# Last 64 queries of two attention heads in one block of 128 rows

## The chip, the cores and the metric

The kernel runs on one core of one Trainium2 chip. The metric is the time of one execution in microseconds (us). The kernel before takes 1045.41 us, the median of three runs (1045.2 to 1045.7).

## The reference

Attention with a decay bias feeds two MLPs. There are 4 batches, 8 heads, 576 positions and 64 channels per head.

```python
cum = np.cumsum(np.maximum(s, 0.0), axis=-1)
bias = -(cum[:, :, :, None] - cum[:, :, None, :])
scores = np.where(causal, -1e9, scale * q @ k.T + np.minimum(bias, 0.0))
attn = np.exp(scores - max); attn = attn / (attn.sum(-1) + 1e-9)
x = (attn @ v) as 2304 tokens of 512
h = x @ w_in;  g = maximum(h, 0) + log1p(exp(-abs(h)));  x = g @ w_out
h = x @ w_in2; g = P(h) / (Q(h) + 1e-6);                 out = g @ w_out2
```

P is a cubic and Q a quadratic in h and |h|; each MLP is 512 to 2048 to 512.

## The kernel before

**Order of the work.** The two MLPs are cut into units of one token tile and 128 of the 2048 inner columns. The first MLP has six token tiles T=0 to 5 (`T1`: 256, 256 and four of 448 tokens), the second six of 384. A loop over the units (L1269) issues for each unit the first product (`stage_a`, L1006 to L1008: three matmuls per 128 rows, since every operand is split into a high and a low part), the nonlinearity (`stage1` to `stage3`), and three units later the second product (`stage_b`, L1042 to L1044 in the first MLP, L1049 to L1051 in the second). Attention runs between the units: `gap` spreads a list of attention steps (`stream`) over the units, in four groups (`GROUPS`), so that each token tile of the first MLP has its attention rows before it starts. Attention ends just before T=4.

**Who sets the order.** All instructions of the first 600 us are put in order, engine by engine, by a planner (`Planner`, `plan`, L1335): a list scheduler over modelled durations that takes the time by which an operation must be done as its rank. What is issued later keeps the order of the tile framework.

**Attention of one head.** A part of kind H (there are 32, one per head and batch) covers queries 384 to 575 of a head, in two blocks of softmax rows. The first (`s1`) is queries 384 to 511, 128 rows against 512 keys. The second (`s2`) is queries 448 to 575, 128 rows against 576 keys, of which only the last 64 rows are used. The parts of kinds L, M and B cover earlier queries. For the second block of one head:

- `scores` (L609, L610) makes two blocks of 288 keys in two PSUM banks, two matmuls each;
- `softmax_rows` adds the mask and takes the row minimum of the negated scores in two DVE operations (L593, L596), the exponent with its row sum on ACT (L600, 128x576), the reciprocal in two small DVE operations (L601, L602) and the scaling on POOL (L603, 128x576), all in the tile `P4`, of which there is one buffer;
- `t2` turns rows 64 to 127 by five transposes of 64 rows (L694), and `evac_pt` takes them from PSUM to SBUF: for batch 0 by one DVE copy (L657), for the others as a high part on ACT (L660) and a low part on DVE (L661);
- `pv` (L732) multiplies by the values and adds the result to the tile of tokens (L743, or L746 and L747).

The turned rows lie in two pairs of tiles `pth`, `ptl` (or `pt` for batch 0), taken in turn by the number of the part (`p.idx % 2`).

```python
for i, k0 in enumerate((448, 0, 128, 256, 384)):
    nc.tensor.transpose(bk[:, (i + 1) * 64:(i + 2) * 64], p.p2[64:128, k0:k0 + 128], ident[64:128, 64:128])
```

**PSUM.** There are eight banks: four for the sums (`acc`), two for `stage_a` (`h`) and two for attention (`at`). `hsel` (L1013) gives the units of T=4 and of most of the second MLP the `h` and `at` banks in turn.

The order of the steps in `stream`, for part number i: load of part i+2, `s1` of i, `pv` of i-2, preparation of the next part, `t1` and `t2` of i-1, `s2` of i.

Of the kernel before, what the change touches and what calls it, by code (L numbers as in the profile page):

```python
# [23 lines left out]
NF = DFF // 128  # L24
# [7 lines left out]
H_ONLY = 5  # L32
# [299 lines left out]
def moe_chain_kernel(ctx, tc, qk0, v0, qk, vv, s0, s, w1, w2, ab, out):  # L332
    nc = tc.nc
# [11 lines left out]
        return sb.tile(shape, dt, tag="W", bufs=NF, name=name)  # L345

    def t_j(name, shape, dt):
        return sb.tile(shape, dt, tag="J", bufs=4, name=name)

    def t_r(name, shape, dt):  # L350
        return sb.tile(shape, dt, tag="R", bufs=2, name=name)
# [1 line left out]
    def t_l(name, shape, dt):  # L353
        return sb.tile(shape, dt, tag="Lw", bufs=8, name=name)
# [10 lines left out]
    def tmp_tile(tag, bufs, shape=(128, TMAX), dt=F32):  # L365
        return sb.tile(list(shape), dt, tag=tag, bufs=bufs, name=tag)
# [13 lines left out]
    def f(ap):  # L380
        return ap.bitcast(F32)
# [4 lines left out]
    abt, nega, babs, qc = prm[:, 0:6], prm[:, 6:10], prm[:, 10:12], prm[:, 12:13]  # L386


    pt_h, pt_l = [], []
    x_t = {}  # L390
    v_t = {}
    raw_t = {}
# [2 lines left out]
    class Part:  # L395
        def __init__(self, b, h, kind, rng, first, plain, pv_plain):
            self.b, self.h, self.kind, self.rng = b, h, kind, rng
            self.fresh, self.first, self.plain, self.pv_plain = rng is not None, first, plain, pv_plain

    def cols(t, rng):  # L400
        if rng[0] == "pre":
# [182 lines left out]
    def softmax_rows(pt, bk, q0, n, stat, i, second=None):  # L584
        mo = 512 - n
        if second is None:
            nc.vector.tensor_tensor_reduce(  # L587
                out=pt[:, 0:n], in0=bk[:, 0:n], in1=mask[:, mo:mo + n], scale=-0.125,
                scalar=3.0e38, op0=ALU.add, op1=ALU.min, accum_out=stat[:, i, 0:1])
            mn = stat[:, i, 0:1]  # L590
        else:
            hn = n // 2
            nc.vector.tensor_tensor_reduce(  # L593
                out=pt[:, 0:hn], in0=bk[:, 0:hn], in1=mask[:, 0:hn], scale=-0.125,
                scalar=3.0e38, op0=ALU.add, op1=ALU.min, accum_out=stat[:, i, 3:4])
            nc.vector.tensor_tensor_reduce(  # L596
                out=pt[:, hn:n], in0=second[:, 0:hn], in1=mask[:, 512 - hn:512], scale=-0.125,
                scalar=stat[:, i, 3:4], op0=ALU.add, op1=ALU.min, accum_out=stat[:, i, 0:1])
# [12 lines left out]

    at_bank = [lambda: bank("at")]

    def abank():
        return at_bank[0]()
# [22 lines left out]
    def s2(p):  # L638
        if p.kind in "LB":
            p.p2 = p_tile(p, "gl")  # L640
            bk = abank()
            scores(bk[:, 0:384], p, 256, 0, 384)
            softmax_rows(p.p2, bk, 256, 384, p.stat, 2)
        elif p.kind == "H":
            p.p2 = tmp_tile("P4", 1, (128, S))
            bk = abank()
            scores(bk[:, 0:288], p, 448, 0, 288)
            bk2 = abank()
            scores(bk2[:, 0:288], p, 448, 288, 288)
            softmax_rows(p.p2, bk, 448, 576, p.stat, 1, second=bk2)  # L650
# [12 lines left out]
    def t1(p):  # L663
        if p.pv_plain:
            p.pt = (sb.tile([128, 960], F32, tag="pt", bufs=2, name="pt"),)
        else:
            p.pt = (pt_h[p.idx % 2], pt_l[p.idx % 2])
        if p.kind == "B":
            return
        bk = abank()  # L670
        if p.kind in "LM":
            for i, c0 in enumerate((256, 0, 128)):
                nc.tensor.transpose(bk[:, i * 128:(i + 1) * 128], p.p1[:, c0:c0 + 128], ident)
            evac_pt([t[:, 0:384] if p.first else t[:, 192:576] for t in p.pt], bk[:, 0:384], nc.scalar)
        else:
            for c in range(4):
                nc.tensor.transpose(bk[:, c * 128:(c + 1) * 128], p.p1[:, c * 128:(c + 1) * 128], ident)
            o = 64 if p.pv_plain else 256
            evac_pt(
                [t[:, o:o + 768].rearrange("p (c q) -> p c q", c=4)[:, :, 0:128] for t in p.pt],  # L680
                bk.rearrange("p (c q) -> p c q", c=4), nc.scalar)

    def t2(p):
        if p.kind == "M":
            return
        bk = abank()
        if p.kind in "LB":
            for i in range(3):
                nc.tensor.transpose(bk[:, i * 128:(i + 1) * 128], p.p2[:, i * 128:(i + 1) * 128], ident)
            evac_pt([t[:, 0:384] if p.pv_plain else t[:, 576:960] for t in p.pt], bk[:, 0:384])  # L690
        else:
# [3 lines left out]
            evac_pt(  # L695
                [t.rearrange("p (c q) -> p c q", c=5)[:, :, 0:64] if p.pv_plain else
                 t[:, 64:1024].rearrange("p (c q) -> p c q", c=5)[:, :, 128:192] for t in p.pt],
                bk[:, 64:384].rearrange("p (c q) -> p c q", c=5))

    def pv(p):  # L700
        if p.first:
            pv_first(p)
            return
        bk = abank()
        hd = p.h % 2
        ops = []
# [66 lines left out]
    }  # L773

    def parts_of(lst, first=False, plain=False, pv_plain=False):
        return [Part(b, h, k, r, first, plain, pv_plain) for b, heads, kind in lst for h in heads for k, r in SPLIT[kind]]

    R8 = range(8)
    segs = [
# [15 lines left out]
    n = 0  # L795
# [131 lines left out]
    def home2(ff, half):  # L927
        if ff >= 14:
            return t_l("w2h", [128, 512], F32R), t_l("w2l", [128, 512], F32R)
        if ff not in w2_t:  # L930
            al = t_j if ff < 2 else t_q if ff < 5 else t_v if ff < 6 else t_w
# [79 lines left out]
    hcnt = [0]  # L1011

    def hsel(ph, T, ff):  # L1013
        if (ph == 0 and T != 4) or (ph == 1 and T == 0 and ff < H_ONLY):
            return "h"
        hcnt[0] += 1
        return ("h", "at")[hcnt[0] % 2]

    def open_acc(ph, T):
        both = ph == 0 and T < 2  # L1020
        n = 2 if both else KD if ph == 0 else TILES[ph][T][1] // 128
        tags = ("at", "at", "acc", "acc") if (ph, T) == (0, 5) else ("acc",) * n
        acc_t[ph, T] = [bank(t) for t in tags]
        if both:
            for a in acc_t[ph, T]:
                nc.tensor.matmul(a, pt_h[0][:, 0:128], w1_t[0][:, 0:512], start=True, stop=False)

    def stage_b(u):
        ph, T, ff = u
# [68 lines left out]
    def stage1_(u):  # L1098
# [11 lines left out]
        else:  # L1110
            a = tmp_tile("e", 2)[:, 0:n]
            t = tmp_tile("PA", 3, (128, n))
            w = tmp_tile(*(("P4", 1), ("tc", 3), ("tmp", 1), ("tc", 3))[(T * NF + ff) % 4], (128, n))
# [36 lines left out]
    if True:  # L1150
# [118 lines left out]
        for i in range(NU + LAGS[1]):  # L1269
# [42 lines left out]
            if u is not None:  # L1312
                gap(i, 1)
                t4 = i - 4 * NF
                if t4 == 0:
                    for lst in (pt_h, pt_l, v_t, op_t, allp, stream):
                        lst.clear()
                if 0 < t4 <= 20:
                    conv2_to(t4)
# [76 lines left out]
```

## Time and profile before

| what | value |
|---|---|
| median of three runs | 1045.41 us |
| the profiled execution | 1044.85 us |
| its span in the profile | 1043.1 us |
| PE busy | 98% of the span |
| ACT, DVE, POOL busy | 77%, 75%, 44% of the span |
| granted TensorE clock | full speed (2.4 GHz) in all 40 slices |

PE is TensorE's matmuls, PEld its weight loads, DVE VectorE, ACT ScalarE, POOL GpSimd. The span is from the first to the last instruction of the profile; 1.75 us of the profiled execution lie outside it. Matmuls are pipelined, and their ends in the profile are modelled: the time that one takes from its engine is read from start to start.

### The profile page before, as it was taken

The numbers are of one execution on the slowest core, as the hardware profiler recorded it, in microseconds if no ns is written. First come the engines' busy times: TensorE is split into PE (matmuls) and PEld (weight loads), VectorE is DVE, ScalarE is ACT, GpSimd is POOL, SyncE is SP. The second block draws the span as 40 slices with busy tenths as digits, with TensorE's granted clock in tenths as the row PEclk, the third lists the DMA queues.
The fourth block names the chain that finished last, engine by engine and source line by source line (L and its number), as shares of the span: only waits on it lengthen the run. The fifth ranks groups of instructions, "written<-read, shape, count | busy, mean of one in ns | idle before, by whom it ended". The sixth has DMA issues, their size and how long they took to land.

```text
span 1043.1 us, 17736 instructions
## 1 busy us (share of the span) xinstructions
PE 1018.0 (98%) x5764; PEld 923.3 (89%) x5764; DVE 784.5 (75%) x1858; ACT 803.5 (77%) x1693; POOL 459.4 (44%) x509
## 2 busy tenths in 40 slices
PE   6999999999999999999999999999999999999998
PEld 5889989988998888999999999989999999999996
DVE  5888877788887888885776787687676776767765
ACT  5898878887887778786566567778787887887875
POOL 2756765421221122222435775445454454444542
PEclk9999999999999999999999999999999999999999
DMA  8877566565564644435779865010010110100100
GB/s 237 298 244 240 171 211 209 176 202 155 167 180 129 207 151 139 129 107 175 246 231 324 301 181 194 1 31 31 1 62 1 31 31 1 44 18 1 31 1 31
DMA packets 67950, 138.70 MB, mean 133 GB/s; under 512 B 8336, under 2 KB 21456, under 8 KB 67856
## 3 DMA queue, kind: packets, MB, share of 16 engines
q1 hardware_dynamic: 65312, 133.39, 40.6%
q10 hardware_dynamic: 2544, 4.16, 1.5%
q8 instruction: 46, 0.75, 0.3%
q14 instruction: 48, 0.39, 0.1%
HBM read 110.82 MB, written 22.61 MB: 128 GB/s over the span
## 4 chain that ended last, share of the span: by engine, by line
PE 71%; DVE 12%; ACT 6%; DMA 4%; POOL 3%; issue 3%; SPq 0%; POOLq 0%; DVEq 0%; ACTq 0%
PE h L1007 6%; PE h L1006 6%; PE h L1008 6%; PE at L732 5%; PE acc L1049 5%; PE acc L1051 5%; PE acc L1050 5%; PE acc L1043 4%; PE acc L1042 4%; PE acc L1044 4%; PE at L1006 3%; PE at L1007 3%; PE at L1008 3%; PE at L609 3%; PE at L610 2%
## 5 line engine op out<-in xcount | busy, mean ns | idle before, releaser
L1006 PE MATMUL h<-xs,w1h 128*128 128x448 f32 (+1 forms) x352 | 120.1, 342 | 1.3 <-DVE e L1108 1.3
L1043 PE MATMUL acc<-gl,w1h 128*128 128x448 f32 (+1 forms) x352 | 119.4, 341 | 1.2 <-POOL gl L1146 1.2
L1007 PE MATMUL h<-xs,w1h 128*128 128x448 f32 (+1 forms) x352 | 119.5, 340 | 0.0
L1008 PE MATMUL h<-xs,w1l 128*128 128x448 f32 (+1 forms) x352 | 119.4, 340 | 0.0
L1042 PE MATMUL acc<-gh,w1h 128*128 128x448 f32 (+1 forms) x352 | 119.3, 341 | 0.0
L1044 PE MATMUL acc<-gh,w1l 128*128 128x448 f32 (+1 forms) x352 | 118.2, 338 | 0.1
L603 POOL TENSOR_SCALAR PA<-PA,stat 128x384 f32<-128x384 f32 (+3 forms) x112 | 71.9, 648 | 101.5 <-DVE stat L602 33.6
L1049 PE MATMUL acc<-w2h,gh 128*128 128x512 f32 x288 | 113.9, 395 | 0.1
L1051 PE MATMUL acc<-w2h,gl 128*128 128x512 f32 x288 | 113.5, 394 | 0.0
L1050 PE MATMUL acc<-w2l,gh 128*128 128x512 f32 x288 | 113.5, 394 | 0.0
L1146 POOL TENSOR_TENSOR gl<-PA,gh 128x384 fp32r<-128x384 f32 x95 | 96.7, 1018 | 6.2 <-ACT gh L1144 5.0
L1117 POOL TENSOR_TENSOR tc<-tc,e 128x384 f32<-128x384 f32 x47 | 50.8, 1082 | 98.5 <-ACT tc L1115 98.5
L603 POOL TENSOR_SCALAR P<-P,stat 128x576 f32<-128x576 f32 x32 | 26.4, 824 | 136.2 <-DVE stat L602 36.0
L600 ACT ACTIVATE PA<-PA,stat 128x384 f32<-128x384 f32 (+3 forms) x112 | 64.0, 572 | 11.5 <-DVE stat L587 9.3
L1006 PEld LDWEIGHTS h<-xs,w1h 128*128 128x128 f32 x352 | 66.3, 189 | 5.4 <-DVE e L1108 1.7
L1043 PEld LDWEIGHTS acc<-gl,w1h 128*128 128x128 f32 x352 | 66.1, 188 | 4.7 <-POOL gl L1146 1.4
L1007 PEld LDWEIGHTS h<-xs,w1h 128*128 128x128 f32 x352 | 66.2, 188 | 3.3
L1008 PEld LDWEIGHTS h<-xs,w1l 128*128 128x128 f32 x352 | 66.2, 188 | 3.3
L1044 PEld LDWEIGHTS acc<-gh,w1l 128*128 128x128 f32 x352 | 66.1, 189 | 3.4 <-POOL w1l L882 0.3
L1042 PEld LDWEIGHTS acc<-gh,w1h 128*128 128x128 f32 x352 | 66.1, 189 | 3.2
L1051 PEld LDWEIGHTS acc<-w2h,gl 128*128 128x128 f32 x288 | 54.1, 188 | 13.1 <-DVE gl L1146 0.3
L1130 DVE SCALAR_TENSOR_TENSOR tc<-tc,e 128x384 f32<-128x384 f32 x48 | 27.5, 574 | 50.4 <-ACT e L1129 48.6
(235 smaller groups left out, 3209.0 us busy)
## 6 DMA issues: line engine op xcount, KB each, us to landing
w1l<-l_d SPq DMA_DIRECT2D x138, 256.0 KB
raw<-in_w_dram SPq DMA_DIRECT2D x48, 512.0 KB
raw<-in_qk_dram SPq DMA_DIRECT2D x24, 384.0 KB
l_d<-w1l SPq DMA_DIRECT2D x32, 256.0 KB
raw64x<-in_w_dram SPq DMA_DIRECT2D x16, 512.0 KB
raw<-in_qk_dram SPq DMA_DIRECT2D x8, 576.0 KB
w_d<-PA SPq DMA_DIRECT2D x16, 256.0 KB
R<-in_vv_dram SPq DMA_DIRECT2D x12, 320.0 KB
```

The lines of the kernel that those rows point to most:

```text
L600: nc.scalar.activation(pt[:, 0:n], pt[:, 0:n], AF.Exp, bias=mn, scale=-1.0, accum_out=stat[:, i, 1:2])
L603: nc.gpsimd.tensor_scalar(pt[:, 0:n], pt[:, 0:n], stat[:, i, 2:3], 1.0, op0=ALU.mult, op1=ALU.mult)
L1006: nc.tensor.matmul(h, wh[:, cs], xh, start=(k == 0), stop=False)
L1007: nc.tensor.matmul(h, wh[:, cs], xl, start=False, stop=False)
L1008: nc.tensor.matmul(h, wl[:, cs], xh, start=False, stop=(k == KD - 1))
L1042: nc.tensor.matmul(o, wh[:, cs], gh, start=first and not both, stop=False)
L1043: nc.tensor.matmul(o, wh[:, cs], gl, start=False, stop=False)
L1044: nc.tensor.matmul(o, wl[:, cs], gh, start=False, stop=last and (not both or m % 2 == 1))
L1049: nc.tensor.matmul(acc[m], gh[:, cs], wh, start=first, stop=False)
L1050: nc.tensor.matmul(acc[m], gh[:, cs], wl, start=False, stop=False)
L1051: nc.tensor.matmul(acc[m], gl[:, cs], wh, start=False, stop=last)
L1146: eng.tensor_tensor(gl, g, f(gh), op=ALU.subtract)
```

## The change

The even head of a pair puts its queries 512 to 575 in rows 0 to 63 of a block, and the odd head its own in rows 64 to 127 of the same block. Each head still has its own four score matmuls and two mask operations, the latter on its 64 rows alone. The exponent, the reciprocal, the scaling and the transposes are done once for both heads; the five transposes take all 128 rows, four into one bank and one into another. `pv` of the even head is done with that of the odd one. The tiles `pth`, `ptl` and `pt` hold both heads (`p.h % 2`); `P4` has two buffers instead of one. The first four units of T=4 take only `h` banks.

```diff
@@ fill
-        for i in range(2):
-            for lst, nm in ((pt_h, "pth"), (pt_l, "ptl")):
-                t = t_j(nm, [128, 1024], F32R)
-                nc.gpsimd.memset(f(t[:, 0:192]), 0.0)
-                lst.append(t)
+        for lst, nm in ((pt_h, "pth"), (pt_l, "ptl")):
+            t = t_j(nm, [128, 2, 1024], F32R)
+            nc.gpsimd.memset(f(t[:, :, 0:192]), 0.0)
+            lst.append(t)
@@ softmax_rows
             hn = n // 2
+            r = slice(0, 64) if q0 == 512 else slice(64, 128)
+            mo = q0 - hn - 64 if q0 == 512 else 512 - hn
             nc.vector.tensor_tensor_reduce(
-                out=pt[:, 0:hn], in0=bk[:, 0:hn], in1=mask[:, 0:hn], scale=-0.125,
-                scalar=3.0e38, op0=ALU.add, op1=ALU.min, accum_out=stat[:, i, 3:4])
+                out=pt[r, 0:hn], in0=bk[r, 0:hn], in1=mask[r, 0:hn], scale=-0.125,
+                scalar=3.0e38, op0=ALU.add, op1=ALU.min, accum_out=stat[r, i, 3:4])
...
             mn = stat[:, i, 0:1]
+            if q0 == 512:
+                return
@@ scores
-        nc.tensor.matmul(o, p.ht[:, 0, q0:q0 + 128], p.ht[:, 1, k0:k0 + n], start=True, stop=False)
-        nc.tensor.matmul(o, p.st[0:68, 0, q0:q0 + 128], p.st[0:68, 1, k0:k0 + n], start=False, stop=True)
+        hq, sq = (t.rearrange("p a s -> p (a s)")[:, q0:q0 + 128] for t in (p.ht, p.st))
+        nc.tensor.matmul(o, hq, p.ht[:, 1, k0:k0 + n], start=True, stop=False)
+        nc.tensor.matmul(o, sq[0:68], p.st[0:68, 1, k0:k0 + n], start=False, stop=True)
@@ s2
-            p.p2 = tmp_tile("P4", 1, (128, S))
+            if p.mate is None:
+                p.p2 = tmp_tile("P4", 2, (128, S))
+                p.stat2 = sb.tile([128, 1, 4], F32, tag="stat2", bufs=2, name="stat2")
+            else:
+                p.p2, p.stat2 = p.mate.p2, p.mate.stat2
+            q0 = 512 if p.mate is None else 448
             bk = abank()
-            scores(bk[:, 0:288], p, 448, 0, 288)
+            scores(bk[:, 0:288], p, q0, 0, 288)
...
@@ t1
-            p.pt = (pt_h[p.idx % 2], pt_l[p.idx % 2])
+            p.pt = (pt_h[0][:, p.h % 2], pt_l[0][:, p.h % 2])
@@ t2
-            for i, k0 in enumerate((448, 0, 128, 256, 384)):
-                nc.tensor.transpose(bk[:, (i + 1) * 64:(i + 2) * 64], p.p2[64:128, k0:k0 + 128], ident[64:128, 64:128])
...
+        elif p.mate is not None:
+            n, ts = (0, pt_p) if p.pv_plain else (128, (pt_h[0], pt_l[0]))
...
+            bk = abank()
+            for i in range(4):
+                nc.tensor.transpose(bk[:, i * 128:(i + 1) * 128], p.p2[:, i * 128:(i + 1) * 128], ident)
+            evac_pt([t[:, :, 1:5] for t in ts], bk.rearrange("p (c j q) -> p j c q", c=4, j=2))
+            bk = abank()
+            nc.tensor.transpose(bk[:, 0:128], p.p2[:, S - 128:S], ident)
+            evac_pt([t[:, :, 0] for t in ts], bk[:, 0:128].rearrange("p (j q) -> p j q", j=2))
@@ pv
+        if p.kind == "H":
+            if p.mate is None:
+                return
+            pv_later(p.mate)
+        pv_later(p)
@@ hsel
-        if (ph == 0 and T != 4) or (ph == 1 and T == 0 and ff < H_ONLY):
+        if (ph == 0 and (T != 4 or ff < 4)) or (ph == 1 and T == 0 and ff < H_ONLY):
             return "h"
```

The rest of the diff follows from these: `t_j` has two buffers of twice the size, the weights `w2` of the second MLP that later take their place are cut in the same way, and `parts_of` gives each odd head its mate.

## Rows read from the trace of the kernel before

**Rows 1.** Page, busy time and share of the span, instructions.

```profile
PE 1018.0 (98%) x5764; PEld 923.3 (89%) x5764; DVE 784.5 (75%) x1858; ACT 803.5 (77%) x1693; POOL 459.4 (44%) x509
```

**Rows 2.** Busy time by stretch: stretch, length, engines' busy us, clock, DMA share, GB/s.

```profile
0.00:60.00 60.00, 47.55 (x265) 40.12 (x266) 41.76 (x178) 44.18 (x129) 31.82 (x57) 1.00 0.86 266
60.00:200.00 140.00, 133.26 (x1043) 127.93 (x1042) 113.00 (x309) 117.49 (x279) 84.20 (x85) 1.00 0.63 201
200.00:476.00 276.00, 275.92 (x1665) 246.52 (x1664) 226.98 (x714) 221.71 (x505) 63.80 (x102) 1.00 0.53 158
476.00:620.00 144.00, 144.00 (x713) 133.03 (x712) 98.26 (x139) 84.94 (x158) 75.55 (x69) 1.00 0.80 258
```

**Rows 3.** Waits of PE from 60 to 200 us: total us, times, longest.

```profile
PE at L689 <- POOL PA L603: 3.0, 5, 0.8
PE at L694 <- POOL P L603: 2.5, 4, 1.1
```

**Rows 4.** Timeline of PE around one group of five transposes of 64 rows.

```profile
212.10 0.36 PE L1008 MATMUL h<-xs,w1l 128*128 128x448 f32 x1
212.30 0.36 PE L1006 MATMUL h<-xs,w1h 128*128 128x448 f32 x1
212.59 0.52 PE L694 MATMUL at<-ident,P 64*128 64x64 f32 x5
213.04 0.47 PE L1007 MATMUL h<-xs,w1h 128*128 128x448 f32 x1
213.35 0.37 PE L1008 MATMUL h<-xs,w1l 128*128 128x448 f32 x1
```

**Rows 5.** Timeline of PE around four transposes of 128 rows, and around one.

```profile
217.17 0.60 PE L677 MATMUL at<-ident,PA 128*128 128x128 f32 x4
217.52 0.45 PE L1008 MATMUL h<-xs,w1l 128*128 128x448 f32 x1
217.81 0.36 PE L1006 MATMUL h<-xs,w1h 128*128 128x448 f32 x1
...
299.21 0.36 PE L1008 MATMUL h<-xs,w1l 128*128 128x448 f32 x1
299.42 0.27 PE L689 MATMUL at<-ident,PA 128*128 128x128 f32 x1
299.44 0.42 PE L609 MATMUL at<-ht 128*128 128x384 f32 x1
299.70 0.34 PE L610 MATMUL at<-st 68*128 68x384 f32 x1
299.88 0.38 PE L689 MATMUL at<-ident,PA 128*128 128x128 f32 x2
```

**Rows 6.** Groups by line, PE: the transposes of 64 rows; count, busy us, mean ns.

```profile
L694 PE MATMUL at<-ident,P 64*128 64x64 f32 x160 | 17.6, 234 | 2.7 <-POOL P L603 2.5
```

**Rows 7.** Groups by line, 60 to 476 us: the other engines' operations around the block.

```profile
L603 POOL TENSOR_SCALAR P<-P,stat 128x576 f32<-128x576 f32 x32 | 26.4, 824 | 136.2 <-DVE stat L602 36.0 <-DVE stat L601 32.8 <-PE at L677 21.3
L600 ACT ACTIVATE P<-P,stat 128x576 f32<-128x576 f32 x32 | 24.5, 765 | 1.9 <-DVE stat L596 1.3 <-ACT ht L564 0.5
L602 DVE RECIPROCAL stat<-stat 128x1 f32<-128x1 f32 x128 | 19.2, 155 | 1.5
L601 DVE TENSOR_SCALAR stat<-stat 128x1 f32<-128x1 f32 x127 | 17.8, 145 | 5.8 <-ACT PA L600 4.3 <-ACT P L600 0.2
L661 DVE TENSOR_TENSOR ptl<-at,pth 128x512 fp32r<-128x512 f32 x24 | 16.5, 688 | 4.2 <-ACT pth L660 3.5
L660 ACT ACTIVATE pth<-at 128x512 fp32r<-128x512 f32 x24 | 14.3, 596 | 1.2 <-PE at L677 0.6
L747 DVE TENSOR_TENSOR x<-at,tmp 64x192 f32<-64x192 f32 x23 | 8.0, 349 | 0.5 <-ACT tmp L746 0.2
L746 ACT ACTIVATE tmp<-at 64x192 f32<-64x192 f32 x23 | 7.5, 326 | 2.3 <-PE at L732 1.8
```

**Rows 8.** Timeline of PE: the first matmul of T=4, next after attention's last.

```profile
476.87 0.37 PE L1006 MATMUL at<-xs,w1h 128*128 128x448 f32 x1
```

More of the change, by code (lines that the diff above doesn't have):

```diff
@@ L347, in t_j @@
     def t_j(name, shape, dt):
-        return sb.tile(shape, dt, tag="J", bufs=4, name=name)
+        return sb.tile(shape, dt, tag="J", bufs=2, name=name)
     def t_r(name, shape, dt):
@@ L592, in softmax_rows @@
             hn = n // 2
+            r = slice(0, 64) if q0 == 512 else slice(64, 128)
+            mo = q0 - hn - 64 if q0 == 512 else 512 - hn
             nc.vector.tensor_tensor_reduce(
-                out=pt[:, 0:hn], in0=bk[:, 0:hn], in1=mask[:, 0:hn], scale=-0.125,
-                scalar=3.0e38, op0=ALU.add, op1=ALU.min, accum_out=stat[:, i, 3:4])
+                out=pt[r, 0:hn], in0=bk[r, 0:hn], in1=mask[r, 0:hn], scale=-0.125,
+                scalar=3.0e38, op0=ALU.add, op1=ALU.min, accum_out=stat[r, i, 3:4])
             nc.vector.tensor_tensor_reduce(
-                out=pt[:, hn:n], in0=second[:, 0:hn], in1=mask[:, 512 - hn:512], scale=-0.125,
-                scalar=stat[:, i, 3:4], op0=ALU.add, op1=ALU.min, accum_out=stat[:, i, 0:1])
+                out=pt[r, hn:n], in0=second[r, 0:hn], in1=mask[r, mo:mo + hn], scale=-0.125,
+                scalar=stat[r, i, 3:4], op0=ALU.add, op1=ALU.min, accum_out=stat[r, i, 0:1])
             mn = stat[:, i, 0:1]
+            if q0 == 512:
+                return
         nc.scalar.activation(pt[:, 0:n], pt[:, 0:n], AF.Exp, bias=mn, scale=-1.0, accum_out=stat[:, i, 1:2])
@@ L644, in s2 @@
         elif p.kind == "H":
-            p.p2 = tmp_tile("P4", 1, (128, S))
+            if p.mate is None:
[4 more added lines that the diff above has]
+            q0 = 512 if p.mate is None else 448
             bk = abank()
-            scores(bk[:, 0:288], p, 448, 0, 288)
+            scores(bk[:, 0:288], p, q0, 0, 288)
             bk2 = abank()
-            scores(bk2[:, 0:288], p, 448, 288, 288)
-            softmax_rows(p.p2, bk, 448, 576, p.stat, 1, second=bk2)
+            scores(bk2[:, 0:288], p, q0, 288, 288)
+            softmax_rows(p.p2, bk, q0, 576, p.stat2, 0, second=bk2)
     def evac_pt(dst, src, eng=None):
@@ L664, in t1 @@
         if p.pv_plain:
-            p.pt = (sb.tile([128, 960], F32, tag="pt", bufs=2, name="pt"),)
+            if not pt_p:
+                pt_p.append(sb.tile([128, 2, 960], F32, name="pt"))
+            p.pt = (pt_p[0][:, p.h % 2],)
         else:
-            p.pt = (pt_h[p.idx % 2], pt_l[p.idx % 2])
+            p.pt = (pt_h[0][:, p.h % 2], pt_l[0][:, p.h % 2])
         if p.kind == "B":
@@ L690, in t2 @@
             evac_pt([t[:, 0:384] if p.pv_plain else t[:, 576:960] for t in p.pt], bk[:, 0:384])
-        else:
-            for i, k0 in enumerate((448, 0, 128, 256, 384)):
-                nc.tensor.transpose(bk[:, (i + 1) * 64:(i + 2) * 64], p.p2[64:128, k0:k0 + 128], ident[64:128, 64:128])
[L695 to L698, printed above, removed]
+        elif p.mate is not None:
+            n, ts = (0, pt_p) if p.pv_plain else (128, (pt_h[0], pt_l[0]))
+            ts = [t[:, :, 0:960] if p.pv_plain else t[:, :, 64:1024] for t in ts]
+            ts = [t.rearrange("p j (c q) -> p j c q", c=5)[:, :, :, n:n + D] for t in ts]
+            bk = abank()
[5 more added lines that the diff above has]
+            evac_pt([t[:, :, 0] for t in ts], bk[:, 0:128].rearrange("p (j q) -> p j q", j=2))
     def pv(p):
@@ L775, in parts_of @@
     def parts_of(lst, first=False, plain=False, pv_plain=False):
-        return [Part(b, h, k, r, first, plain, pv_plain) for b, heads, kind in lst for h in heads for k, r in SPLIT[kind]]
+        out, mates = [], {}
+        for b, heads, kind in lst:
+            for h in heads:
+                for k, r in SPLIT[kind]:
+                    p = Part(b, h, k, r, first, plain, pv_plain)
+                    p.mate = mates.get((b, h - 1, k)) if h % 2 else None
+                    mates[b, h, k] = p
+                    out.append(p)
+        return out
     R8 = range(8)
@@ L929, in home2 @@
             return t_l("w2h", [128, 512], F32R), t_l("w2l", [128, 512], F32R)
+        if ff < 2 and ff not in w2_t:
+            t = t_j("w2", [128, 2, 1024], F32R)
+            w2_t[ff] = (t[:, 0], t[:, 1])
         if ff not in w2_t:
-            al = t_j if ff < 2 else t_q if ff < 5 else t_v if ff < 6 else t_w
+            al = t_q if ff < 5 else t_v if ff < 6 else t_w
             w2_t[ff] = (al("w2h", [128, 1024], F32R), al("w2l", [128, 1024], F32R))
@@ L1025, in open_acc @@
             for a in acc_t[ph, T]:
-                nc.tensor.matmul(a, pt_h[0][:, 0:128], w1_t[0][:, 0:512], start=True, stop=False)
+                nc.tensor.matmul(a, pt_h[0][:, 0, 0:128], w1_t[0][:, 0:512], start=True, stop=False)
     def stage_b(u):
@@ L1315, in moe_chain_kernel @@
                 if t4 == 0:
-                    for lst in (pt_h, pt_l, v_t, op_t, allp, stream):
+                    for lst in (pt_h, pt_l, pt_p, v_t, op_t, allp, stream):
                         lst.clear()
```

6 lines of the change are left out of this document (4 added, 2 removed).

## The prediction

> **What bounds the kernel now.** I read the page's busy shares first, then busy time by stretch, then PE's own waits, then PE's timeline around single groups of transposes. The page shows PE busy 98% of the span, the next engine 77% [rows 1]. Such a share is an average, so the stretches decide [rows 2]. In the first 60 us PE is busy 47.55 us and the DMA engines 0.86: that is the start, and the loads bound it. From 60 to 200 us PE is busy 133.26 of 140 us while ACT (117.49) and DVE (113.00) are nearly full too: a mixed bound, in which PE waits now and then, mostly for POOL's scaled rows ahead of a transpose, 3.0 and 2.5 us in all [rows 3]. From 200 to 476 us PE is busy 275.92 of 276 us and waits for nothing, though DVE and ACT have 49 and 54 us to spare. So from 200 us on only what leaves PE's own queue shortens the kernel. The clock is full in every stretch.
>
> A busy PE says little of what one matmul costs it, since records overlap. So the price of a transpose is read from start to start, with the matmuls on both sides.
>
> **The change part by part.**
>
> *Transposes of 64 rows, removed.* The matmuls of 448 columns start 0.20 us apart (212.10, 212.30) [rows 4]. From the start of the last one before the group (212.30) to the start of the second one after it (213.35) are 1.05 us. Two matmuls of 448 columns take 0.40 of that, so the five transposes cost PE 0.65 us. Of this, 0.45 lies between the first transpose and the next matmul; the rest is that the matmul before is followed 0.09 us late (0.29 in place of 0.20) and the one after 0.11 late (0.31). There are 160 such transposes [rows 6], so 32 groups of five: 32 x 0.65 = 20.8 us.
>
> *Transposes of 128 rows, added.* The same reading [rows 5]: four of them start at 217.17, the second matmul after them at 217.81; less one matmul of 448 columns that is 0.44 us. One alone: from 299.21 to 299.70 are 0.49 us, of which a matmul of 448 columns takes 0.20 and one of 384 columns 0.18 (299.70 to 299.88): 0.11 us. The change puts four in one bank and one in another, 16 times: 16 x (0.44 + 0.11) = 8.8 us. The difference is **12.0 us of PE time**: 9.0 in the 24 heads (12 pairs) of batches 1 to 3, which lie behind 200 us where PE bounds alone, and 3.0 in the 8 heads of batch 0, before. For an unseen group I bound it from both sides: if the lone transpose of each pair costs as much as a quarter of the four (0.11) nothing moves; if the plan splits the pair's transposes so that each piece pays the 0.20 us on its two sides that the 64-row group shows [rows 4], 16 x 0.20 = 3.2 us are lost; if half of the groups of 64 rows are split in the kernel before and cost 0.20 more, 3.2 us more are won. I take the middle, since around transposes of all 128 rows no such cost is seen [rows 5].
>
> The price is not one per column [rows 4, 5]: five transposes with 320 columns cost 0.65 us, four with 512 columns 0.44. The Trainium skill (TensorE: Matmul & The Clock Gate, section Back-to-back issue gap) gives a gap of columns / 2.4 + 2.5 ns at the full clock. By that rule ten transposes of 64 columns and five of 128 would take 0.29 and 0.28 us, an estimate from that page, and the change would give PE 0.2 us in all. By this the trace does not go, and the rule returns as a rival.
>
> *Score matmuls, value matmuls.* Each head keeps its four score matmuls with 288 columns, and `pv` its ten matmuls. The score weights now begin at query 512 for the even head and are still 128 columns wide. No cost.
>
> *Exponent, reciprocal, scaling.* Per pair one of each goes: ACT 16 x 0.765 = 12.2 us, DVE 16 x (0.145 + 0.155) = 4.8, POOL 16 x 0.824 = 13.2 [rows 7]. Behind 200 us they lie beside PE work and are worth nothing. In batch 0 they stand in the chain to a transpose that PE waits for: four of its waits, 2.5 us, are for the block that is now halved [rows 3]. Half of them would be 1.2 us; as the pair's block also needs the second head's scores, I take half of that, **0.6 us**, with ends of 0 and 5.5 us (both rows of waits gone).
>
> *Mask operations on 64 rows.* As many operations with as many columns. DVE's time may stay or fall to half; it lies beside PE either way. I take no gain.
>
> *Evacuation.* Before, two of 320 columns per pair; now one of 512 (ACT 0.596, DVE 0.688 [rows 7]) and one of 128, which by the nearest rows, of 192 columns, takes at most 0.326 and 0.349. Together 0.92 and 1.04 us; below it the ends are the 512 ones alone. Both lie beside PE.
>
> *Moved `pv`, shared tiles.* The even head's ten value matmuls start one step later. Behind them on PE stand the next transposes, and their readers are the splits of the next token tile, which come several units later. A part of kind L or B and the H part of the same head now share a tile, so H's evacuation must come after the earlier `pv`; PE runs that ahead of H's transposes anyway, so the wait is over when it begins. No DMA is added or moved, on SP, ACT or POOL. Per pair there are as many `at` banks as before (twelve), two of them shorter.
>
> *T=4 in `h` banks for four units.* Before, its first matmul stood in an `at` bank, right behind attention's last matmuls [rows 8], and so needed a bank that attention had left. T=3, with the same 448 columns, lives on two `h` banks within the stretch where PE is never idle [rows 2]. I take zero, with ends of 0.5 us either way. The zero fill on POOL and the tiles of `w2` change their shape, not their size.
>
> **Sum.** 12.0 + 0.6 = 12.6 us. The profiled execution took 1044.85 us, 1043.1 of it span; 12.6 less is 1032.25. The median of the runs stands 0.56 us above that execution, so the median after is **1032.8 us**. 0.2% of the kernel, about 2.1 us, is what a measurement of it can tell from no change.
>
> **Rivals.**
>
> 1. *The gain before 200 us is not paid out*, since ACT, DVE and POOL bound the stretch as much as PE does. For it: ACT 117 and DVE 113 of 140 us [rows 2]. Against it: they are relieved as well. Then only 9.0 us are won: 1036.4 us. Chance 0.13.
> 2. *The waits for POOL in that stretch go with the relief*, both rows of them, 5.5 us [rows 3]: 12.0 + 5.5 = 17.5 won, 1027.9 us. Against it: half of them are for other blocks, which stay. Chance 0.11.
> 3. *PE's time for a transpose goes by its columns*, ten of 64 being five of 128: PE wins nothing, the change does not do what it says, and 0.6 us of waits are left: 1044.8 us, no change. The row that speaks against it is the 0.65 beside the 0.44 us. Chance 0.05.
> 4. *The pair's work comes in a burst that the two `at` banks can't take*, the one way to be slower. Within one step PE has the five transposes and twenty value matmuls of both heads, in four banks where there are two; the first `pv` waits until a bank of transposes is evacuated (0.596 + 0.688), the second until a `pv` is (0.326 + 0.349): at most 1.96 us per pair [rows 7], 31 us in all. It decides from 12.6 / 16 = 0.79 us per pair; at 1.2 us it would cost 19.2 us and give 1052 us. Against it: today the banks go round as fast and PE stands still nowhere behind 200 us [rows 2], because the plan puts MLP matmuls between. Chance 0.05.
>
> **How the numbers follow.** The forecast has a chance of 0.66. Its own ends are 12.6 less 3.2 and plus 3.2, so 1029.6 to 1036.0. The range of 1027 to 1038 holds the forecast, rival 1 with 1.6 us to spare and rival 2 with 0.9; outside are rivals 3 and 4 and the tails of a plan that is made anew, some 0.2 in all. Faster by over 0.2% are the forecast and rivals 1 and 2: 0.90. Within 0.2% is rival 3: 0.05. Slower is rival 4: 0.05.
>
> **What would show it.** In the profile after, the transposes of a P block should be 80 of 128 rows, the exponent and scaling of 128x576 should be 16 each, and from start to start a group of four should cost 0.44 us and a lone one 0.11, with no late start on either side. The first matmul of T=4 should come about 12 us sooner, some 9 of them from the stretch behind 200 us, and PE should still be filled there. From T=4 on the two kernels should run alike. I am wrong if PE shows waits for `at` banks (for L660, L661, L746 or L747) behind 200 us, if the stretch before 200 us is not shorter, or if the groups of 128 rows pay the 0.2 us on their sides.

## The result, and the profile after

The changed kernel takes 1036.34 us (median of four runs, 1035.01 to 1037.7), beside 1045.31 us for the kernel before on the same chip: 0.9916 of it, with a 95% interval of 0.9904 to 0.9929. That is 9.0 us where 12.6 were forecast: inside the range, a little below the forecast's own low end (9.4), and in size what rival 1 gave (1036.4), though not for its reason, as the stretches show.

The page of the profiled execution (1035.79 us, 1033.6 of it span) has PE at the same share as before [rows 1], with 80 matmuls fewer:

```profile
PE 1011.0 (98%) x5684; PEld 917.0 (89%) x5684; DVE 785.7 (76%) x1826; ACT 791.2 (77%) x1661; POOL 448.1 (43%) x491
```

Busy time by stretch, columns as in [rows 2]:

```profile
60.00:200.00 140.00, 135.85 (x1041) 129.78 (x1040) 118.40 (x313) 117.87 (x276) 81.48 (x83) 1.00 0.65 211
200.00:476.00 276.00, 275.16 (x1628) 246.18 (x1627) 224.98 (x680) 213.98 (x485) 55.70 (x88) 1.00 0.54 163
```

Before 200 us PE is fuller than it was (135.85 beside 133.26 us); behind 200 us it is no longer quite full (275.16 beside 275.92 of 276). That last 0.84 us is the first sign that something other than PE shows through.

The block itself became what the diff says. Groups by line, 60 to 476 us: scaling and exponent 16 times instead of 32 [rows 7], and the transposes of the pair, 16 times four and 16 times the fifth, instead of 160 [rows 6]:

```profile
L607 POOL TENSOR_SCALAR P<-P,stat 128x576 f32<-128x576 f32 x16 | 12.8, 800 | 72.4 <-DVE stat L606 44.7 <-ACT e L1137 6.1 <-ACT PA L604 5.8
L604 ACT ACTIVATE P<-P,stat 128x576 f32<-128x576 f32 x16 | 12.4, 772 | 4.4 <-DVE stat L598 4.2
L709 PE MATMUL at<-ident,P 128*128 128x128 f32 x64 | 10.0, 278 | 0.9 <-POOL P L607 0.9
L712 PE MATMUL at<-ident,P 128*128 128x128 f32 x16 | 4.5, 279 | 0.0
```

Timeline of PE around one pair's transposes:

```profile
219.47 0.36 PE L1041 MATMUL h<-xs,w1l 128*128 128x448 f32 x1
219.67 0.60 PE L709 MATMUL at<-ident,P 128*128 128x128 f32 x4
220.11 0.27 PE L712 MATMUL at<-ident,P 128*128 128x128 f32 x1
220.13 0.45 PE L1075 MATMUL acc<-gh,w1h 128*128 128x448 f32 x1
220.42 0.36 PE L1076 MATMUL acc<-gl,w1h 128*128 128x448 f32 x1
```

The matmul before is followed on time (0.20 us), and from 219.47 to 220.42 are 0.95 us, less 0.40 for the two matmuls of 448 columns: 0.55 us for the pair, as forecast, where two heads cost 1.30 [rows 4]. The matmul behind the fifth starts 0.03 us after it (220.106 and 220.134 in the trace) and is itself followed after 0.29 us, as behind the four in [rows 5]; the 0.55 holds both.

**Where the time went.** Three matmuls mark the stretches: the first of the first MLP, the first of T=2 and the first of the second MLP. Timeline of PE of the kernel before:

```profile
31.15 0.39 PE L1006 MATMUL h<-xs,w1h 128*128 128x256 f32 x1
...
197.12 0.37 PE L1006 MATMUL h<-xs,w1h 128*128 128x448 f32 x1
...
624.92 0.34 PE L1006 MATMUL h<-yt,w2h 128*128 128x384 f32 x1
```

and of the changed kernel:

```profile
30.27 0.39 PE L1039 MATMUL h<-xs,w1h 128*128 128x256 f32 x1
...
193.85 0.37 PE L1039 MATMUL h<-xs,w1h 128*128 128x448 f32 x1
...
615.72 0.34 PE L1039 MATMUL h<-yt,w 128*128 128x384 f32 x1
```

| stretch | before | after | difference |
|---|---|---|---|
| to the first MLP matmul | 31.15 | 30.27 | -0.9 |
| A: from there to T=2 | 165.97 | 163.58 | -2.4 |
| B: T=2 to the second MLP | 427.80 | 421.87 | -5.9 |
| the rest of the span | 418.18 | 417.88 | -0.3 |

The first line is no effect of the change: a kernel that runs in the order of the kernel before (e10, below) also begins 0.8 us earlier. The last line is nothing. Stretch A holds batch 0's four pairs, stretch B the other twelve.

A and B do not hold quite the same work in the two kernels, since the planner made the order anew. Busy time in stretch A by line, first the scores (L609, then L614), then the value matmuls (L732, then L754), each before and after:

```profile
31.15:197.12 165.97, 16.88 (x42) 7.91 (x42) 1.00 0.67 218
30.27:193.85 163.58, 16.78 (x44) 8.30 (x44) 1.00 0.67 219
31.15:197.12 165.97, 25.71 (x170) 24.23 (x170) 1.00 0.67 218
30.27:193.85 163.58, 26.32 (x176) 24.70 (x176) 1.00 0.67 219
```

With the second score line (L610, then L615: again 42 and 44) four score and six value matmuls have come from B into A. From start to start they take 0.74 and 0.58 us, 1.3 together. **At equal work, then, 3.7 us were won in A and 4.6 in B.**

Against this stands what the block's transposes cost, read from start to start as in the prediction and summed over their groups, waits included: in A 8.57 us before and 3.52 after, in B 16.84 and 7.55. **So 5.1 us were saved there in A and 9.3 in B, and 3.7 and 4.6 came out.** In B most of the rest is in late starts of PE outside these groups. There are seven of over 0.15 us, 2.1 us together, where the kernel before has none; and those of 0.05 to 0.15 us are 51 instead of 28, some 2 us more. Five of the seven lie at attention's end. Waits of PE in the changed kernel, 430 to 480 us (total us, times, longest; the last one is in the groups' 7.55):

```profile
PE at L754 <- ACT pth L670: 0.4, 1, 0.4
PE at L754 <- DVE stat L598: 0.2, 1, 0.2
PE at L709 <- POOL P L607: 0.2, 1, 0.2
```

The largest is for an operation that the change itself brings. Timelines of PE and of ACT around it:

```profile
468.48 0.33 PE L712 MATMUL at<-ident,P 128*128 128x128 f32 x1
...
469.92 0.37 PE L1041 MATMUL h<-xs,w1l 128*128 128x448 f32 x1
470.68 0.85 PE L754 MATMUL at<-pth,vs 128*128 128x256 f32 x5 [0.39 <-ACT pth L670]
```

```profile
468.62 0.60 ACT L670 ACTIVATE pth<-at 128x512 fp32r<-128x512 f32 x1 [0.29 <-PE at L709]
469.92 0.54 ACT L1137 ACTIVATE e<-h 128x448 f32<-128x448 f32 x1 [0.70 <-PE h L1041]
470.36 0.27 ACT L670 ACTIVATE pth<-at 128x128 fp32r<-128x128 f32 x1
```

The lone fifth transpose is done at 468.8, but its evacuation stands on ACT behind an MLP operation that itself waits for PE, and begins at 470.36; the value matmuls of the pair need it and start 0.56 us late.

### The profile page after: what moved, and what is told of

Same layout as the page of the kernel before. It is cut to its first block, busy times and chain, and to the rows that moved or that the text cites. A ratio compares the mean times of both kernels' runs of the same rounds, so it can differ in the third digit from the quotient of the medians.

```text
span 1033.6 us, 17441 instructions
## 1 busy us (share of the span) xinstructions
PE 1011.0 (98%) x5684; PEld 917.0 (89%) x5684; DVE 785.7 (76%) x1826; ACT 791.2 (77%) x1661; POOL 448.1 (43%) x491
## 4 chain that ended last, share of the span: by engine, by line
PE 76%; DVE 9%; ACT 5%; DMA 4%; POOL 4%; issue 3%; SPq 1%; POOLq 0%; DVEq 0%; ACTq 0%
PE h L1039 7%; PE h L1040 7%; PE h L1041 7%; PE at L754 6%; PE acc L1082 5%; PE acc L1084 5%; PE acc L1083 5%; PE acc L1077 4%; PE acc L1075 4%; PE acc L1076 4%; PE at L1039 3%; PE at L1040 3%; PE at L1041 3%; PE at L614 3%; PE at L615 2%
## 5 line engine op out<-in xcount | busy, mean ns | idle before, releaser
L607 POOL TENSOR_SCALAR PA<-PA,stat 128x384 f32<-128x384 f32 (+3 forms) x112 | 72.9, 657 | 165.1 <-DVE stat L606 65.7
L1039 PE MATMUL h<-xs,w1h 128*128 128x448 f32 (+1 forms) x360 | 122.8, 342 | 1.6 <-DVE e L1141 1.5
L1040 PE MATMUL h<-xs,w1h 128*128 128x448 f32 (+1 forms) x360 | 122.6, 341 | 0.0
L1041 PE MATMUL h<-xs,w1l 128*128 128x448 f32 (+1 forms) x360 | 122.3, 340 | 0.0
L1082 PE MATMUL acc<-w2h,gh 128*128 128x512 f32 x252 | 99.6, 395 | 0.1
L1084 PE MATMUL acc<-w2h,gl 128*128 128x512 f32 x252 | 99.3, 394 | 0.0
L1083 PE MATMUL acc<-w2l,gh 128*128 128x512 f32 x252 | 99.2, 394 | 0.0
L1039 PEld LDWEIGHTS h<-xs,w1h 128*128 128x128 f32 x360 | 67.9, 189 | 5.7 <-DVE e L1141 2.4
L1040 PEld LDWEIGHTS h<-xs,w1h 128*128 128x128 f32 x360 | 67.8, 188 | 3.7 <-DVE xs L1009 0.4
L1137 ACT ACTIVATE e<-h 128x448 f32<-128x448 f32 (+1 forms) x90 | 43.4, 483 | 33.5 <-PE h L1041 31.6
L1177 ACT ACTIVATE gh<-PA 128x384 fp32r<-128x384 f32 x96 | 50.4, 525 | 20.9 <-DVE PA L1165 17.7
```

The source lines that it names most:

```text
L1039: nc.tensor.matmul(h, wh[:, cs], xh, start=(k == 0), stop=False)
L1040: nc.tensor.matmul(h, wh[:, cs], xl, start=False, stop=False)
L1041: nc.tensor.matmul(h, wl[:, cs], xh, start=False, stop=(k == KD - 1))
L1082: nc.tensor.matmul(acc[m], gh[:, cs], wh, start=first, stop=False)
L1083: nc.tensor.matmul(acc[m], gh[:, cs], wl, start=False, stop=False)
L1084: nc.tensor.matmul(acc[m], gl[:, cs], wh, start=False, stop=last)
```

## The experiments

All ratios are to the kernel before, run on the same chip in turn with it, with 95% intervals. A and B are the stretches of the table above, from one profile each; the start of a kernel before its first MLP matmul differs by some 1 us from run to run, which A and B leave out. In every new order (all runs but e2, e3 and e10) the 1.3 us of work lie in A instead of B. In e4, e8, e9 and e13 the granted clock was at the lower level for 3.4 us inside A, so their A is too long by up to 1.7 us, an estimate from half the clock over that time.

| kernel | median us | ratio | A | B |
|---|---|---|---|---|
| before | 1043.68 to 1045.31 | 1 | 165.97 | 427.80 |
| changed | 1036.34 | 0.9916 (0.9904 to 0.9929) | 163.58 | 421.87 |
| e1, T=4 banks back | 1038.24 | 0.9935 (0.9913 to 0.9956) | 163.80 | 422.82 |
| e2, T=4 banks only | 1044.62 | 0.9997 (0.9986 to 1.0008) | 165.48 | 428.49 |
| e3, lower rows | 1044.46 | 1.0004 (0.9995 to 1.0014) | 166.32 | 427.66 |
| e4, ten transposes | 1043.77 | 1.0001 (0.9992 to 1.0010) | 168.32 | 425.39 |
| e5, two exponents | 1050.01 | 1.0049 (1.0037 to 1.0061) | 165.02 | 424.88 |
| e7, another plan of before | 1049.43 | 1.0055 (1.0035 to 1.0076) | 166.37 | 431.37 |
| e8, value matmuls apart | 1034.96 | 0.9910 (0.9894 to 0.9927) | 165.71 | 421.17 |
| e9, another plan of the change | 1039.49 | 0.9948 (0.9934 to 0.9963) | 164.94 | 422.71 |
| e10, full rows in the old order | 1058.90 | 1.0144 (1.0127 to 1.0161) | 168.89 | 439.39 |
| e11, eight h units | 1037.06 | 0.9933 (0.9919 to 0.9947) | 163.87 | 422.45 |
| e13, apart and eight h units | 1034.63 | 0.9905 (0.9891 to 0.9919) | 164.34 | 420.85 |
| e12, apart and all h units | 1032.52 | 0.9893 (0.9878 to 0.9908) | 162.70 | 421.22 |

My theory: the gain is PE's time in the transposes, and part of it is given back in the order that the planner makes anew. The rivals: the gain is the relief of ACT, DVE and POOL; or part of it is the banks of T=4.

**e3: are 64 rows dear, or the upper 64?** The kernel before with its used queries in rows 0 to 63. The planner gives the same order, instruction for instruction.

```diff
-            scores(bk[:, 0:288], p, 448, 0, 288)
+            scores(bk[:, 0:288], p, 512, 0, 288)
...
-                nc.tensor.transpose(bk[:, (i + 1) * 64:(i + 2) * 64], p.p2[64:128, k0:k0 + 128], ident[64:128, 64:128])
+                nc.tensor.transpose(bk[:, (i + 1) * 64:(i + 2) * 64], p.p2[0:64, k0:k0 + 128], ident[0:64, 0:64])
```

> The kernel before, each head alone, with its queries 512 to 575 in rows 0 to 63 of its block instead of rows 64 to 127, so the five transposes of 64 rows take their rows from the lower half. If the 0.65 us of such a group comes from a matmul on part of the rows as such, it stays 0.65 us and the time 1045 us within 1.5. If it comes from the upper half, the group falls to about 0.31 to 0.45 us and the time to 1035 to 1039 us.

Same time, and the same group (timeline of PE of e3):

```profile
212.21 0.36 PE L1008 MATMUL h<-xs,w1h 128*128 128x448 f32 x1
212.50 0.52 PE L696 MATMUL at<-ident,P 64*128 64x64 f32 x5
212.95 0.47 PE L1009 MATMUL h<-xs,w1h 128*128 128x448 f32 x1
213.26 0.36 PE L1010 MATMUL h<-xs,w1l 128*128 128x448 f32 x1
```

Again 1.05 us less 0.40, so 0.65: half the rows are dear wherever they lie.

**e4: the transposes undone, the rest of the change kept.** Each head's five transposes take their own 64 rows, into a bank of their own.

```diff
-            for i in range(4):
-                nc.tensor.transpose(bk[:, i * 128:(i + 1) * 128], p.p2[:, i * 128:(i + 1) * 128], ident)
...
+            for j, r in enumerate((slice(0, 64), slice(64, 128))):
+                bk = abank()
+                for i, k0 in enumerate((448, 0, 128, 256, 384)):
+                    nc.tensor.transpose(bk[:, i * 64:(i + 1) * 64], p.p2[r, k0:k0 + 128], ident[r, r])
+                evac_pt([t[:, j] for t in ts], bk[:, 0:320].rearrange("p (c q) -> p c q", c=5))
```

> The change with the exponent and scaling shared but the transposes undone: ten of 64 rows per pair, five from rows 0 to 63 into one bank and five from rows 64 to 127 into another. If the gain is PE's time in the transposes, it is gone: 1045 to 1048 us, and from the first matmul of T=2 to that of the third quarter of T=4 (where the change is 5.9 us shorter than the kernel before) within 1.5 us of the kernel before. If the gain is the relief of ACT, DVE and POOL, 1036 to 1038 us.

The gain is gone (1.0001), so relief alone does not make it. B is 2.4 us shorter than before, 1.1 at equal work, inside the 1.5 I allowed; A is 2.4 us longer, no more than the moved work and the lower clock account for. But its groups cost less than before, 11.95 us instead of 16.84 in B, and the timeline of PE of e4 says why:

```profile
225.45 0.36 PE L1037 MATMUL h<-xs,w1h 128*128 128x448 f32 x1
225.75 0.65 PE L710 MATMUL at<-ident,P 64*128 64x64 f32 x10
226.32 0.47 PE L1038 MATMUL h<-xs,w1h 128*128 128x448 f32 x1
226.63 0.37 PE L1039 MATMUL h<-xs,w1l 128*128 128x448 f32 x1
```

Ten transposes in one run cost 1.18 - 0.40 = 0.78 us, where five cost 0.65. They come from both halves, and some start only 0.007 us apart, so this run does not part the price of a transpose from that of a run. The order of e7 (below) does, since it splits many of the groups of the kernel before. A lone transpose of 64 rows (timeline of PE of e7):

```profile
434.12 0.34 PE L610 MATMUL at<-st 68*128 68x384 f32 x1
434.40 0.27 PE L694 MATMUL at<-ident,P 64*128 64x64 f32 x1
434.60 0.47 PE L1043 MATMUL acc<-gl,w1h 128*128 128x448 f32 x1
434.91 0.37 PE L1044 MATMUL acc<-gh,w1l 128*128 128x448 f32 x1
```

From 434.12 to 434.91 are 0.79 us, less 0.18 and 0.20 for the matmuls on its sides: 0.41. Runs of two, three, four and five cost 0.47, 0.52, 0.58 and 0.65 in e7 (medians). **So what is dear is not the transpose of 64 rows, 0.06 us, but the way into a run of them and out of it, 0.35 us once.** On the way in the run starts 0.09 us late (0.29 behind the matmul before, in place of 0.20); on the way out the next matmul starts 0.15 us after the last transpose, where it is 0.03 behind one of 128 rows. The 0.31 that the prediction counted as late behind the run says less: behind 128 rows it is 0.29.

**e10: full rows in the old order.** This holds the order fixed and changes only the price. The kernel before, each head alone; the five transposes become five matmuls of all 128 rows with half of the identity.

```diff
-                nc.tensor.transpose(bk[:, (i + 1) * 64:(i + 2) * 64], p.p2[64:128, k0:k0 + 128], ident[64:128, 64:128])
+                nc.tensor.matmul(bk[:, (i + 1) * 64:(i + 2) * 64], p.p2[:, k0:k0 + 128], ident[:, 64:128], start=True, stop=True)
```

> The kernel before in its own order, instruction for instruction, each head alone; only the five transposes of 64 rows become five matmuls of all 128 rows with columns 64 to 127 of the identity, so PE no longer goes to part of its rows and back. If the 0.65 us of a group is that going there and back, the group falls to 0.30 to 0.45 us, and since the order is unchanged, what comes out in the end shows how much of saved PE time is paid out: all of it (6 to 11 us, 1033 to 1038 us) if PE bounds throughout, three quarters of it if the stretch before 200 us is bound by other engines as well. If the price lies in the number of transposes and not in their rows, the group stays at 0.55 to 0.65 us and the time within 2 us of the kernel before.

I missed the price: slower by 15 us. Each such matmul runs as two, so the profile has ten per group (timeline of PE of e10):

```profile
222.75 0.36 PE L1008 MATMUL h<-xs,w1l 128*128 128x448 f32 x1
222.96 1.22 PE L694 MATMUL at<-ident,P 128*128 128x64 f32 x10
223.99 0.45 PE L1042 MATMUL acc<-gh,w1h 128*128 128x448 f32 x1
224.27 0.36 PE L1043 MATMUL acc<-gl,w1h 128*128 128x448 f32 x1
```

The group costs 1.52 - 0.40 = 1.12 us, ten at 0.11. The way in is free (0.21), as expected of full rows. What the run was for came out all the same, with the sign turned. Its marks (timeline of PE):

```profile
30.32 0.39 PE L1006 MATMUL h<-xs,w1h 128*128 128x256 f32 x1
...
199.20 0.37 PE L1006 MATMUL h<-xs,w1h 128*128 128x448 f32 x1
...
638.60 0.34 PE L1006 MATMUL h<-yt,w2h 128*128 128x384 f32 x1
```

In B the groups cost 28.14 us instead of 16.84, 11.3 more, and B is 439.39 - 427.80 = 11.6 us longer. In A they cost 4.1 more and A is 2.9 longer. **At a fixed order PE's time is paid in full behind 200 us, and to some seven tenths before**; the seven tenths are rough, since A differs by 0.8 us between e2 and e3, which run alike there.

**e5: exponent, reciprocal and scaling once per head again**, on its own 64 rows; the transposes stay shared.

```diff
             mn = stat[:, i, 0:1]
-            if q0 == 512:
-                return
+            pt, stat, mn = pt[r], stat[r], mn[r]
```

> The change with the exponent, the reciprocal and the scaling done for each head on its own 64 rows (twice per pair, with as many columns each), the transposes still shared. If the gain is PE's time in the transposes, 1036 to 1038 us, the loss being the waits for POOL before 200 us (0 to 1.2 us). If the gain is the relief of ACT, DVE and POOL, back to 1043 to 1045 us.

Outside both expectations: slower than the kernel before. The stretches part it. 7.5 us of its loss against the changed kernel come before the first MLP matmul, which starts at 37.80 us instead of 30.27: the plan of the start came out otherwise, and PE stood 3.5 us in one wait for POOL there; no exponent of the pair's block has begun by then. Busy time by stretch of e5, with the granted clock at 0.94 in the first 60 us:

```profile
0.00:60.00 60.00, 46.16 (x247) 38.81 (x248) 40.81 (x172) 43.59 (x125) 35.91 (x56) 0.94 0.86 277
```

In B it is 3.0 us longer than the changed kernel. The three longest waits of PE of e5, 470 to 484 us:

```profile
PE at L708 <- POOL P L606: 1.3, 1, 1.3
PE at L753 <- ACT pth L669: 0.8, 1, 0.8
PE at L700 <- POOL PA L606: 0.3, 1, 0.3
```

So the second exponent and scaling are not free at attention's end: the chain from scores to transposes shows there. Elsewhere in B PE starts its transposes at most some 0.3 us late for POOL. The order of e5 is new as well, so the 3.0 us are not theirs alone; but e5 lies 2.1 us above the highest B of an order with one exponent.

**e1 and e2: the banks of T=4.** e1 is the change without this edit, e2 the kernel before with nothing else.

```diff
-        if (ph == 0 and (T != 4 or ff < 4)) or (ph == 1 and T == 0 and ff < H_ONLY):
+        if (ph == 0 and T != 4) or (ph == 1 and T == 0 and ff < H_ONLY):
```

> The change with the four units of T=4 in h and at banks in turn, as in the kernel before; all else as changed. If the h banks let those units slip in ahead of attention's last blocks and so cost the short waits of PE seen between 430 and 476 us (2.2 us), this runs at about 1034 us. If the banks are neutral, 1036.3 within 1 us. If the h banks carry part of the gain, 1038 to 1040 us.

> The kernel before with nothing but the four units of T=4 in h banks. If the gain of the change lies in the transposes, this stays within 1 us of 1045.3. If the banks carry part of the gain, 1042 to 1043 us. If they cost something, 1047 us.

Alone the edit is worth nothing (0.9997; B 0.7 us longer). With the pair it is worth 0.95 us of B in one profile; the whole times (0.9935 beside 0.9916) have overlapping intervals. The h banks do not cost the short waits, as I had suspected. Without them PE waits more, for T=4's tokens to be split and again at value matmuls (waits of PE of e1, 200 to 480 us):

```profile
PE h L1039 <- ACT xs L1008: 0.9, 1, 0.9
PE at L754 <- DVE ptl L671: 0.6, 1, 0.6
```

**e7 and e9: what an order is worth.** e7 is the kernel before with one price of the planner changed; e9 the change without a bank that `t2` asks for and does not use. Neither changes an operation.

```diff
-            self.busy = 0.00085 * n if turn else 0.024 + 0.00162 * n if full else 0.012 + 0.000428 * n
+            self.busy = (0.13 if n == 64 else 0.00085 * n) if turn else 0.024 + 0.00162 * n if full else 0.012 + 0.000428 * n
```

```diff
-        bk = abank()
         if p.kind in "LB":
+            bk = abank()
```

> The kernel before with one number of the planner changed: it reckons a transpose of 64 rows at 0.13 us, as measured, instead of 0.054. No operation changes, only the order. If the kernel before was slow because its plan was made with too low a price, 1041 to 1043 us. If the order matters little, 1044.6 within 1 us. If orders differ at random by a few us, anything from 1042 to 1049 us.

> The change without the bank that the step of the second block of H asks for at its head and never uses. It does the same operations; only the order in which they are planned can differ. If the order that the planner finds is worth a few us either way, this differs from 1036.3 by 1 to 4 us. If the order is worth nothing, 1036.3 within 0.5 us.

e7 loses 5.5 us in the median, though its price is the measured one. The planner now splits more groups: 34 pieces in B where the kernel before has 27, for the same 24 heads, and they cost 20.4 us instead of 16.84, waits included. e9 gives 0.9948 where the change gives 0.9916, some 3 us less. An order found anew is worth some us either way. Over all paired orders with shared transposes and one exponent, B lies between 420.9 and 422.8, or 422.2 and 424.1 with the 1.3 us that went to A, below every unpaired one (427.7 to 428.5, and e7): that part of the gain is not luck. A, less these 1.3 us, lies between 161.4 and 164.4, the unpaired ones, e7 less the same, between 165.1 and 166.3; they do not overlap either, though the three highest of the paired (e8, e9, e13) are those with the lower clock in A.

**e8, e11, e13, e12: the waits that are left.** e8 puts the odd head's value matmuls one step after the even one's. e11 is the change with eight units of T=4 in `h` banks, e13 is e8 with eight, e12 is e8 with all 16.

```diff
         if p.kind == "H":
-            if p.mate is None:
-                return
-            pv_later(p.mate)
+            if p.mate is not None:
+                pv_later(p.mate)
+            return
         pv_later(p)
...
+        a3 = at(i - 3)
+        if a3 is not None and a3.kind == "H" and a3.mate is not None:
+            stream.append((pv_odd, a3))
```

> The change with the value matmuls of the odd head one step later than those of the even one, so that the two no longer come in one step. If the burst of both makes the short waits of PE behind 200 us, 1033 to 1035 us. If the waits have another cause, 1036.3 within 1.5 us.

> The change with the first eight units of T=4 in h banks instead of four; the order differs only around attention's end. If PE's short waits at attention's end (1.6 us of waits over 0.15 us between 439 and 476 us) come from too few MLP matmuls that may run ahead of attention's last blocks, they go: 1034.7 to 1035.5 us. If two h banks are too few for T=4, 1037 to 1040. If neither, 1036.3 within 0.5 us.

> The change with the value matmuls of the odd head one step later, and with eight units of T=4 in h banks. The first alone gave 0.991 of the kernel before. If the waits at attention's end are what is left, 0.9895 to 0.990 of it; if not, 0.991 again; if h banks run short, 0.993 or more.

> The change with the value matmuls of the odd head one step later, and with all 16 units of T=4 in h banks. If two h banks carry a tile of 448 columns without attention beside it, this is as fast as with eight units, 0.9895 to 0.991 of the kernel before. If they don't, each unit waits some tenths of a us and it comes to 0.993 or more.

e8 shortens B by 0.7 us and empties attention's end of all but one wait over 0.15 us, but brings others elsewhere; its whole time is not told apart from the change. e11 is no faster: the three waits of PE at attention's end are all still there, so a lack of MLP matmuls that may run ahead is not their cause. e13 (0.9905) is not told apart from either. e12 is the fastest measured, 0.9893, its upper end (0.9908) just above the lower end of the change (0.9904); B says 0.65 us, and the rest of its lead is in A and the start. There its order is that of e8, whose A is 3.0 us longer with the lower clock in it, so that part is not the work of the edit. So e12 beats the kernel before, and the changed one probably by little. With all 16 units on two `h` banks T=4 is no slower.

## Why the prediction was right, and where it failed

- **The price of a transpose, from start to start: right.** 0.65 us for a group of 64 rows, 0.44 and 0.11 for the pair's. In B 9.3 us were saved at the transposes, beside the 9.0 worked out. One reading was wrong and did no harm: the matmul behind 128 rows is followed late too (0.29 in [rows 5] and after the change), so the sign "no late start on either side" holds only for the side before; the sums of 0.44 and 0.55 include it.
- **That PE bounds behind 200 us and pays one for one: right at a fixed order** (e10: 11.3 at the groups, 11.6 in the stretch).
- **What failed is the step that took the new order at nothing**: the moved value matmuls have no term in the sum, the second evacuation was to "lie beside PE", and with the shared tiles "the wait is over when it begins". In B 4.7 of 9.3 us were given back at equal work, some 4 of them in late starts outside the transposes, the largest for the fifth transpose's evacuation on ACT (0.39 us at L754 for L670, once L660, whose waits the prediction had named as a sign of being wrong). I had put an end of 3.2 us on the forecast for split transposes and unseen groups. The shortfall is 3.6 us and has another cause, so that the time still lies in the range owes something to luck: its upper part was room for rival 1, which is not what happened.
- **"Worth nothing" for the exponent and scaling behind 200 us: mis-sized.** Taken back (e5) they cost up to 3.0 us of B, most of it at attention's end, where the chain of the last heads is no longer covered. The page's 77% for ACT cannot show this.
- **Before 200 us: 5.1 us saved at the transposes and their waits, 3.7 out at equal work**, where 3.6 were forecast: the right sum from wrong terms, 3.0 of price and 2.1 of waits, not all paid. e10's seven tenths say the same: the stretch is mixed, as rival 1 had it, but not that nothing is paid.
- **Rival 2** had the waits right and their worth wrong. Of the 5.5 us of waits for POOL in [rows 3] 0.9 are left (waits of PE in the changed kernel, 60 to 200 us):

```profile
PE at L709 <- POOL P L607: 0.7, 2, 0.5
PE at L701 <- POOL PA L607: 0.2, 1, 0.2
```

  The other waits there rose from 1.1 to 2.5 us, and A paid 3.7 us, not the 8.5 of this rival.
- **Rival 1** has the right total and the wrong place: it lost all before 200 us and nothing behind. **Rival 3**, a price by columns alone, falls by e4 and e10. **Rival 4** is there in kind (value matmuls that wait), with under 0.2 us a pair in B (2.1 us of late starts over 0.15 us, 12 pairs) where 0.79 would have decided, and for an evacuation, not for a bank.
- **T=4 in h banks: zero alone (e2), some 1 us together with the pair (e1)**, a little over the 0.5 allowed, in one profile each. From T=4's third quarter on the kernels run alike (9.2 us sooner there and at the second MLP). The sign of T=4's first matmul rested on a misreading: [rows 8] show its first in an `at` bank, but counted by units T=4 had begun in an `h` bank by 469.31 us, and in the changed kernel, where four units may run ahead of attention's end, by 446.40.

Open: how the 4.7 us divide among order, shared tiles and the second evacuation. A new order alone can be worth as much: e7, unpaired, lost 4.9 us of B at equal work, about half of it in the seven pieces more at 0.35 us each. Tiles of their own for the H parts, which would take one of the three away, were not tried.

## What to carry to other kernels

Read the price of a matmul from start to start with its neighbours, and take what it saves in full only where PE is full and the order stays; where a planner makes the order anew, put an end of several us on it, and measure one or two orders that differ in nothing else. Mark stretches by the work they hold, and count that work on both sides before taking a difference. An operation that is almost always covered may have one place where it isn't: look where its stream ends and the filler work runs out. A kernel that changes the price and keeps the order is the cleanest test of a bound, whichever way the price goes.

## What the hardware showed that was not expected

- **Part of the rows costs on the way in and out.** A run of transposes of 64 rows costs 0.35 us and 0.06 for each transpose (e7), wherever the rows lie (e3); a run of ten from both halves costs 0.78, with pairs as little as 0.007 us apart (e4). The Trainium skill (TensorEngine Tiling (Array Packing), section Tiling Modes) says that a change of the tiling mode drains the engine, and that different tiles can run in parallel. Both agree with these rows: the run starts 0.29 us behind the matmul before in place of 0.20, the next matmul 0.15 behind its last transpose in place of 0.03, and ten cost little more than five. No run here shows that the drain is the cause.
- **An FP32 matmul of 128 rows and 64 columns by the identity is run as two, at 0.11 us each**, so that five take 1.12 us where five transposes of 128 rows and 128 columns take 0.55 (e10).
- **The granted clock is not always full in the first 200 us.** It is 1.00 throughout in the kernel before and the changed one. In e5 it was at the lower of its two levels (1.2 instead of 2.4 GHz) for 6.8 us from 31.0 us on, and fell while PE stood in the wait of 3.5 us for POOL. In e4, e8, e9 and e13 it was there for 3.4 us, from 164.1, 30.4, 61.0 and 30.7 us on; just before or around that PE waited 1.8 us for DVE in e4 and 1.2 for POOL in e9, but at most 0.5 in e8 and e13. Busy time by stretch of e8:

```profile
30.50:33.70 3.20, 3.20 (x13) 2.82 (x13) 2.94 (x4) 2.60 (x8) 3.20 (x5) 0.50 0.62 241
```
